# q and k of eight heads in one DRAM tensor, and three V tiles moved between the scores

## The chip, the cores and the metric

The kernel runs on one core of one Trainium2 chip. The metric is the device time of one execution in microseconds (us), the median of several runs. Engines: TensorE (PE for products, PEld for its weight loads), VectorE (DVE), ScalarE (ACT), GpSimd (POOL), and SyncE (SP), which here only issues DMA transfers. SBUF is the memory on the chip with 128 partitions, PSUM the memory that TensorE writes, in banks of 128 x 512 float32; DRAM is the memory off the chip.

## The reference

The inputs are x (1 x 2048 x 512, float32), and weights for attention (wqkv, wo), for a gated MLP (w1, w3, w2; F = 1792) and for a gate (gate_w):

```
q, k, v = split(x @ wqkv)              # 32 heads of 16
p = softmax(q @ k.T * 16 ** -0.5)      # per head, 2048 x 2048
a = merge(p @ v) @ wo
b = (silu(x @ w1) * (x @ w3)) @ w2
g = sigmoid((x * gate_w).sum(-1))
out = g * a + (1 - g) * b
```

## The kernel before

All products run in a float32 mode with each operand split in a high and a low half, hi and lo, and three products in place of one (hi·hi, hi·lo, lo·hi). Only p·V uses plain float32.

The work has three parts.

**The head.** x is loaded and transposed. `project_qk` computes q and k of the first 128 columns, which are 8 heads of 16 (column group c = 0), in four blocks of 512 rows of x (b = 0 to 3). ScalarE writes hi, VectorE lo, and `store_qk` stores them in DRAM. `project_v` computes a tile of V, 128 rows, with 12 full products. The 16 tiles of V fill the time of TensorE while the last block of q and k goes to DRAM and comes back. `bound` and `guard_rows` work out a bound on the scores, and two more rows for q (m_d) that keep the exponent safe. Then a flag is read by all engines, and a branch (`row_maxima`, line 293) is passed whose body runs only for large scores. The last three tiles of V (13 to 15) are computed ahead of the branch and copied behind it (line 415).

**The loop.** The order of all that TensorE does is written out by hand as a string: Q is a score (for two heads at once, 128 keys x 512 queries each), F a slot of other work, P two blocks of p·V. One period holds 8 scores. `one` has 21 slots F, `two` has 15; LONG and SHORT say how often each is used. There are 32 steps of 32 scores (16 pairs of heads, two halves of the queries). `load_step` fetches q, k and the guard rows of the next step when a step is 6 scores old. Each head's operand has 50 rows: three times 16 for the hi and lo combinations (q: hi, lo, hi; k: hi, hi, lo) and two guard rows. So a step took 3 + 3 fetches for each of two heads, and 2 for the guard rows: 14.

In a slot F, `feed` gives one half product (64 of 128 rows of weights) to each of two lanes, which are the halves of TensorE's array. A block of other work takes 12 or so slots in one lane, then as many in the other, and writes one of three PSUM banks. `blocks` lists the blocks in order: q and k of the column groups 1 to 3 (24 blocks, handled by `qk_done`), the MLP's first layer, its second (`h_product`), and the product with wo for the first half of the rows. When a block is done, `qk_done` copies its bank to a buffer `gs` (VectorE, line 443), and POOL makes hi in `sg` and lo in `gs` (lines 444 and 445); then SP stores both. `gs` and `sg` have two buffers each. `pick` gives a bank to a new block when the block three before it was done at least REST = 7 clock steps ago.

SP issues all DMA transfers in the order of the program. Each uses one of eight semaphores in turn, and waits for the one that used it before.

**The tail.** After the last p·V, what is left of the product with wo is done for the tiles 8 to 15; `mix` (VectorE) or `scaled` (ScalarE and POOL) adds the gated parts, and the rows go out.

Of the kernel before, what the change touches and what calls it, by code (L numbers as in the profile page):

```python
# [17 lines left out]
P = 128  # L18
S = 2048
# [3 lines left out]
DH = 16  # L23
NB = S // 512
# [9 lines left out]
def gated_mix_kernel(ctx: ExitStack, tc: tile.TileContext, x, wqkv, wo, w1, w3, w2, gate_w, out):  # L34
# [27 lines left out]
    qkp = ctx.enter_context(tc.tile_pool(name="qkp", bufs=1))  # L62
    fw = ctx.enter_context(tc.tile_pool(name="fw", bufs=2, side="right"))
# [3 lines left out]
    wvp = ph1.enter_context(tc.tile_pool(name="wvp", bufs=1))  # L67

    QD = [[dram.tile([D, S], F32, name=f"{n}{p}_d") for p in "HL"] for n in "qk"]
# [110 lines left out]
    def x_gate(b):  # L180
        for t in range(4):
            nc.vector.scalar_tensor_tensor(slot("hx", F32), xn[b][:, t, :], 1.0, gw, op0=OP.mult, op1=OP.mult,
                                           accum_out=z[:, 4 * b + t:4 * b + t + 1])

    def store_qk(i, c, b, hi, lo):
        for t, d in zip((hi, lo), QD[i]):
            nc.sync.dma_start(d[P * c:P * c + P, 512 * b:512 * b + 512], t.bitcast(F32) if t.dtype == F32R else t)

    def project_qk(c, b, w, between=None):
        ps = psum2()  # L190
        for i in range(2):
            if i and between:
                between()
            order = [(h, xs, k) for h, xs in ((0, xH), (1, xH), (0, xL)) for k in range(ND)]
            if c == b == i == 0:
                order = [(0, xH, 0), (0, xH, 3), (0, xH, 1), (0, xH, 2), (0, xL, 0), (0, xL, 3),
                         (1, xH, 0), (1, xH, 3), (1, xH, 1), (1, xH, 2), (0, xL, 1), (0, xL, 2)]
            for n, (h, xs, k) in enumerate(order):
                nc.tensor.matmul(ps[:, i, :], w[i][h][:, k, :], xs[b][:, k, :], start=n == 0,  # L199
                                 stop=n == len(order) - 1)  # L200
        hi = p1.tile([P, 2, 512], F32R, name="hi", bufs=2)
        lo = p1.tile([P, 2, 512], F32R, name="lo", bufs=2)
        nc.scalar.activation(hi, ps, AF.Copy)
        nc.vector.tensor_sub(lo, ps, hi)
        for i in range(2):
            store_qk(i, c, b, hi[:, i, :], lo[:, i, :])
# [3 lines left out]
    def load_v():  # L210
        for k in range(ND):
            r = slot(("fh1", "fl1", "fh3", "fl3")[k], F32)
            nc.sync.dma_start(r, wqkv[P * k:P * k + P, 2 * D:3 * D])
            vh, vl = (wvp.tile([P, 512], F32R, name=f"v{n}{k}") for n in "hl")
            nc.gpsimd.tensor_copy(vh, r)
            nc.gpsimd.tensor_sub(vl, r, vh)
            wv.append((vh, vl))
# [46 lines left out]

    def load_k(j, i):
        for h in range(2):
            r = 64 * h
            s = slice(DH * (2 * j + h), DH * (2 * j + h) + DH)
            for o, ks in enumerate((0, 0, 1)):
                nc.sync.dma_start(Kt[i][r + DH * o:r + DH * o + DH, :].bitcast(F32), QD[1][ks][s, :])  # L270

    def load_q(j, half, i):
        for h in range(2):
            r = 64 * h
            s = slice(DH * (2 * j + h), DH * (2 * j + h) + DH)
            for o, qs in enumerate((0, 1, 0)):
                nc.sync.dma_start(Qt[i][r + DH * o:r + DH * o + DH, :].bitcast(F32),
                                  QD[0][qs][s, 1024 * half:1024 * half + 1024])

    def load_guard(j, half, i):  # L280
        for h in range(2):
            nc.sync.dma_start(Qt[i][64 * h + 48:64 * h + 50, :].bitcast(F32),
                              M_d[2 * j + h, :, 1024 * half:1024 * half + 1024])
# [154 lines left out]
    def qk_done(c, i, b):  # L438
        def done(ps):
            nonlocal qk_left  # L440
            lo = slot("gs", F32)
            hi = slot("sg")
            nc.vector.tensor_copy(lo, ps)
            nc.gpsimd.tensor_copy(hi, lo)
            nc.gpsimd.tensor_sub(lo, lo, hi)
            store_qk(i, c, b, hi, lo)
            qk_left -= 1
        return done
# [73 lines left out]
    def load_piece(t, q):  # L522
        if t == 1 and q < 2:
            both = wk.tile([P, 2, 512], F32R, name=f"wo{2 + q}")
            hi, lo = both[:, 0, :], both[:, 1, :]
        else:
            hi, lo = (slot(SETS[t % 2][2 * q + i])[:] for i in range(2))
        tag = "fr" if t == 0 or t == 1 and q < 2 else "sg"
        n = min(4, NF - 4 * q)
        src = h_d[512 * q:512 * q + P * n, P * t:P * t + P].rearrange("(f p) t -> p f t", p=P)  # L530
        halves_of(src, hi[:, 0:P * n], lo[:, 0:P * n], tag)
        hs.setdefault(t, []).append((hi, lo))

    def load_wo(k):
        if k < 2:
            hi, lo = w2H[3][:, 2 + k, :], w2L[3][:, 2 + k, :]
        else:
            both = wk.tile([P, 2, 512], F32R, name=f"wo{k}")
# [66 lines left out]
    def divide(k, half):  # L605

        yield from reciprocals(k, half)
        for b in (2 * half, 2 * half + 1):
            for _ in range(5):
                yield  # L610
            if half == 0:
                o, r = slot("hx", F32), slot("gw", F32)
            else:
                both = wk.tile([P, 2, 512], F32, name="od")
# [12 lines left out]
    def load_bt(t):  # L627
        bt[t] = wk.tile([P, 512], F32, name=f"bt{t % 3}")
# [62 lines left out]
    def six_heads():  # L691
# [9 lines left out]
        both = wk.tile([P, 2, 512], F32, name="od")  # L701
# [13 lines left out]

    def blocks():
# [21 lines left out]
    NBLOCK = 8 * len(chunks) + 3 * NT + NT // 2 + NT // 2  # L738
# [4 lines left out]
    halves = [None, None]  # L743
# [7 lines left out]
    def pick(lane, rest, gap):  # L751
# [3 lines left out]
        if used < 0 or over[used] is not None and over[used] + rest <= clock:  # L755
            block, halves[lane] = halves[lane] or next(source, None), None
            if block:
                if type(block[1]) is tuple:
                    product, done, length = block
                    block, halves[1 - lane] = (product, done[0], length), (product, done[1], length)  # L760
                over.append(None)
                return dict(block=block, ps=bank(), id=len(over) - 1, n=0, turn=None, alone=halves[1 - lane] is not None or len(over) == NBLOCK)
# [78 lines left out]
    LONG, SHORT = 90, 37  # L841
# [7 lines left out]
    for i, c in enumerate(order):  # L849
        clock += 1 if c != "P" else 4  # L850
        if c == "Q":
# [14 lines left out]
            if small or later and hurry:  # L866
                for _ in range(3 if hurry else 1 + (len(small) > (6 if len(over) < 8 * len(chunks) - 16 else 0))):
                    if small or later and hurry:
                        (small or later).pop(0)()
            if loads and (hurry or issued % 2 or len(over) > 8 * len(chunks) - 12):  # L870
                loads.pop(0)()
# [44 lines left out]
    project(last, 1, (0, 1))  # L916
# [8 lines left out]
    project(last, 1, (2,))  # L925
    project(last, 2)

    def scaled(t):
        y = wk.tile([P, 512], F32, name=f"p{free[t // 2 - 3]}")
        nc.scalar.activation(y, banks[t], AF.Copy, scale=g[:, t:t + 1])  # L930
        nc.gpsimd.tensor_add(bt[t], bt[t], y)

    def store(t):
        nc.sync.dma_start(out[P * t:P * t + P, :], bt[t])

    banks[8], banks[9] = one_[:, 1, :], two_[:, 1, :]
    banks[10], banks[11] = bank(), bank()
    for two in ((8, 9), (10, 11), (12, 13), (14,), (15,)):
        if two[0] == 12:
            banks[12], banks[13], banks[14] = psum2()[:, 0, :], psum2()[:, 0, :], acc  # L940
        for terms in ((0, 1), (2,)):
            for t in two:
                project(t, k, terms)
        for t in two:
            if t in (8, 10):
                scaled(t)
            elif t < last:
                mix(t, banks[t], nc.scalar if t % 2 == 0 else nc.sync)
                if t in (9, 11):
                    store(t - 1)  # L950
            else:
                mix(t, banks[t], nc.scalar, slice(0, D // 2))
                mix(t, banks[t], nc.sync, slice(D // 2, D))
# [27 lines left out]
```

## Time and profile before

| | |
|---|---|
| median of 3 runs | 1403.08 us (1402.96 to 1403.56) |
| the profiled execution | 1403.71 us, span of its instructions 1401.9 us |
| TensorE busy | 1393.8 us (99%) |
| ScalarE busy | 1034.3 us (74%) |
| VectorE, POOL busy | 486.9 us (35%), 329.3 us (23%) |
| DMA | 112479 packets, 141.03 MB, 101 GB/s on average |
| granted clock of TensorE | 0.999 |

The profile's page gives the busy time of each engine, then the chain of work that ended last: followed back from the last instruction, at each step to what released it. The chain in order of time lists the same pieces with start and length. A timeline lists instructions with start, length, engine, line, what they write and read, and in brackets the idle time before them with what ended it. A view by line lists its instructions with their shortest, median and longest time in ns, and whom they waited for. A window gives the busy time of each engine between two times, then TensorE's clock, the mean busy share of the 16 DMA engines and what they moved. Queues that issue are written SPq, DVEq and so on.

### The profile page before, as it was taken

The numbers are of one execution on the slowest core, as the hardware profiler recorded it, in microseconds if no ns is written. First come the engines' busy times: TensorE is split into PE (matmuls) and PEld (weight loads), VectorE is DVE, ScalarE is ACT, GpSimd is POOL, SyncE is SP. The second block draws the span as 40 slices with busy tenths as digits, with TensorE's granted clock in tenths as the row PEclk, the third lists the DMA queues.
The fourth block names the chain that finished last, engine by engine and source line by source line (L and its number), as shares of the span: only waits on it lengthen the run. The fifth ranks groups of instructions, "written<-read, shape, count | busy, mean of one in ns | idle before, by whom it ended". The sixth has DMA issues, their size and how long they took to land.

```text
span 1401.9 us, 29019 instructions
## 1 busy us (share of the span) xinstructions
PE 1393.8 (99%) x11497; PEld 826.4 (59%) x11497; DVE 486.9 (35%) x1083; ACT 1034.3 (74%) x1155; POOL 329.3 (23%) x366
## 2 busy tenths in 40 slices
PE   9999999999999999999999999999999999999998
PEld 8866566566566566566566566566555555555554
DVE  5511111564555546555454554511111101111113
ACT  4457677777777777777777777777677887888784
POOL 6123433011011101110110116432344322212312
PEclk9999999999999999999999999999999999999999
DMA  7653554343223423223333236444354453444632
GB/s 209 166 124 94 133 139 113 73 113 77 46 56 85 114 54 76 69 66 93 74 77 74 66 86 165 118 95 91 87 123 105 105 110 77 111 93 110 157 120 78
DMA packets 112479, 141.03 MB, mean 101 GB/s; under 512 B 16276, under 2 KB 70804, under 8 KB 109264
## 3 DMA queue, kind: packets, MB, share of 16 engines
q1 hardware_dynamic: 111616, 137.92, 41.4%
q8 instruction: 93, 1.52, 0.5%
q10 hardware_dynamic: 720, 1.18, 0.2%
q14 instruction: 50, 0.41, 0.1%
HBM read 90.43 MB, written 48.61 MB: 99 GB/s over the span
## 4 chain that ended last, share of the span: by engine, by line
PE 99%; DVE 0%; issue 0%; DVEq 0%
PE acc L817 33%; PE f L432 27%; PE S L829 19%; PE f L550 11%; PE f L634 2%; PE S L199 2%; PE f L641 1%; PE f L96 1%; PE f L98 1%; PE f L97 1%; PE f L165 0%; PE acc L353 0%; PE f L897 0%; PE S L165 0%; PE S L897 0%; DVE xL L646 0%
## 5 line engine op out<-in xcount | busy, mean ns | idle before, releaser
L833 ACT ACTIVATE p<-S 128x1024 f32<-128x1024 f32 x1024 | 967.9, 1026 | 314.1 <-PE S L829 305.0
L817 PE MATMUL acc<-p,V 128*17 128x512 f32 x4096 | 471.5, 594 | 0.0
L829 PE MATMUL S<-Qt,Kt 50*128 50x512 f32 x2048 | 403.7, 407 | 0.8 <-DVE V L415 0.8
L829 PEld LDWEIGHTS S<-Qt,Kt 50*128 50x128 f32 x2048 | 184.0, 184 | 173.5 <-issue 77.7
L817 PEld LDWEIGHTS acc<-p,V 128*17 128x17 f32 x4096 | 103.4, 97 | 275.2 <-issue 275.2
L463 DVE RECIPROCAL sg<-sg 128x64 f32<-128x64 f32 x448 | 209.2, 517 | 52.7 <-issue 49.1
L432 PE MATMUL f<-xH,fl 64*128 64x512 f32 x1088 | 220.6, 395 | 0.0
L432 PE MATMUL f<-xL,fh 64*128 64x512 f32 x1088 | 219.6, 393 | 0.0
L432 PE MATMUL f<-xH,fh 64*128 64x512 f32 x1088 | 218.0, 389 | 0.0
L328 POOL CAST fh<-fr 128x512 fp32r<-128x512 f32 x34 | 22.4, 658 | 428.0 <-DMA fr<-in_B_w_dram 279.6
L432 PEld LDWEIGHTS f<-xH,fh 64*128 64x128 f32 x1088 | 105.6, 184 | 25.0 <-issue 0.4
L432 PEld LDWEIGHTS f<-xL,fh 64*128 64x128 f32 x1088 | 106.4, 186 | 22.5
L432 PEld LDWEIGHTS f<-xH,fl 64*128 64x128 f32 x1088 | 106.1, 186 | 22.7
L789 DVE MEMSET tick<- 1x1 f32 x198 | 11.7, 59 | 281.2 <-PE f L550 143.0
L455 DVE COPY gs<-f 128x512 f32<-128x512 f32 x56 | 38.5, 688 | 65.5 <-PE f L432 59.3
L461 DVE TENSOR_SCALAR sg<-sg 128x512 f32<-128x512 f32 x56 | 27.3, 488 | 88.0 <-ACT sg L460 84.3
L550 PE MATMUL f<-xH,fh 64*128 64x512 f32 x208 | 57.5, 392 | 0.0
L550 PE MATMUL f<-xH,raw 64*128 64x512 f32 x192 | 57.0, 392 | 0.0
L550 PE MATMUL f<-xL,fh 64*128 64x512 f32 x208 | 56.2, 392 | 0.0
L550 PE MATMUL f<-xH,fl 64*128 64x512 f32 x208 | 55.4, 392 | 0.0
L513 POOL CAST fh<-sg 128x512 fp32r<-128x512 f32 (+1 forms) x32 | 18.0, 563 | 147.3 <-DMA sg<-h_d 91.0
L799 DVE COPY u<-acc 128x512 f32<-128x512 f32 x31 | 21.4, 692 | 86.1 <-PE acc L817 86.1
(202 smaller groups left out, 1324.6 us busy)
## 6 DMA issues: line engine op xcount, KB each, us to landing
Kt<-kH_d SPq DMA_DIRECT2D x128, 128.0 KB
h_d<-sg SPq DMA_DIRECT2D x56, 256.0 KB
sg<-h_d SPq DMA_DIRECT2D x43, 256.0 KB
fr<-in_B_w_dram SPq DMA_DIRECT2D x42, 256.0 KB
Qt<-qH_d SPq DMA_DIRECT2D x128, 64.0 KB
Kt<-kL_d SPq DMA_DIRECT2D x64, 128.0 KB
Qt<-qL_d SPq DMA_DIRECT2D x64, 64.0 KB
b_d<-y SPq DMA_DIRECT2D x16, 256.0 KB
```

The lines of the kernel that those rows point to most:

```text
L199: nc.tensor.matmul(ps[:, i, :], w[i][h][:, k, :], xs[b][:, k, :], start=n == 0, stop=n == len(order) - 1)
L328: nc.gpsimd.tensor_copy(hi, src)
L432: return nc.tensor.matmul(ps, w[i == 1][r, k, :], (xL if i == 2 else xH)[b][r, k, :], start=n == 0 and not second, stop=n == 3 * ND - 1 an ...
L455: nc.vector.tensor_copy(gs, ps)
L461: small.append(lambda: nc.vector.tensor_scalar(sg, sg, 1.0, None, op0=OP.add))
L463: small.append(lambda q=q: nc.vector.reciprocal(sg[:, q:q + 64], sg[:, q:q + 64]))
L550: ins = nc.tensor.matmul(ps, hs[t][q][i == 1][r, P * o:P * o + P], (w2L if i == 2 else w2H)[q][r, o, :], start=n == 0 and not second, stop ...
L634: return nc.tensor.matmul(ps, ot[t][i == 1][r, P * k:P * k + P], wo_[k][i == 2][r, :], start=n == 0 and not second, stop=n == 3 * ND - 1 a ...
L799: nc.vector.tensor_copy(u, acc)
L817: nc.tensor.matmul(acc[r:r + DH + 1, :], V[:, k, 2 * j + h, :], p[:, h, :], start=k == 0, stop=k == NT - 1)
L829: nc.tensor.matmul(ps[:, h, :], Kt[i][r:r + 50, P * k:P * k + P], Qt[i][r:r + 50, t:t + 512], start=True, stop=True)
L833: nc.scalar.activation(p, ps, AF.Exp, scale=SCALE)
```

## The change

q and k of 8 heads go to one DRAM tensor for each column group, `QK[i][c]`, ordered by o (0 to 2, the copy), then d (the row in a head, 16), then head (8), then 2048 positions. Copy o holds hi or lo as the operand of the score wants it, so hi is stored twice: three stores of 128 x 512 in place of two. A fetch of a head's 48 rows is then one transfer; a step has 2 for q, 2 for k, and 2 for the guard rows.

The tiles 13 to 15 of V leave the head (EARLY = 13) and become the first blocks of the loop's other work. LONG goes from 90 to 96 and SHORT from 37 to 31. `bound` comes ahead of tile 9, and the fetches of the first step come directly one after another behind the guard rows.

The tiles of wv stay in SBUF and lend their place later (`v0` to `v3`) to tiles that had names of their own (wo2, wo3, od, bt). At the end of the loop, tile 13's part is split in the two lanes as tile 14's was, the last three blocks may take a bank after 3 steps instead of 7, and the tail's tiles 8 to 15 are computed and mixed one by one, all on VectorE.

```diff
-    QD = [[dram.tile([D, S], F32, name=f"{n}{p}_d") for p in "HL"] for n in "qk"]
+    QK = [[dram.tile([3, DH, 8, S], F32, name=f"{n}{c}_d") for c in range(ND)] for n in "qk"]
...
-    def store_qk(i, c, b, hi, lo):
-        for t, d in zip((hi, lo), QD[i]):
-            nc.sync.dma_start(d[P * c:P * c + P, 512 * b:512 * b + 512], t.bitcast(F32) if t.dtype == F32R else t)
+    def store_qk(i, c, b, half, t):
+        for o, low in enumerate(((0, 1, 0), (0, 0, 1))[i]):
+            if low == half:
+                nc.sync.dma_start(QK[i][c][o, :, :, 512 * b:512 * b + 512].rearrange("d h t -> h d t"),
+                                  t.bitcast(F32) if t.dtype == F32R else t)
...
+    def rows_of(i, hh):
+        return QK[i][hh // 8].rearrange("o d h t -> (o d) h t")[:, hh % 8, :]
+
     def load_k(j, i):
         for h in range(2):
-            r = 64 * h
-            s = slice(DH * (2 * j + h), DH * (2 * j + h) + DH)
-            for o, ks in enumerate((0, 0, 1)):
-                nc.sync.dma_start(Kt[i][r + DH * o:r + DH * o + DH, :].bitcast(F32), QD[1][ks][s, :])
+            nc.sync.dma_start(Kt[i][64 * h:64 * h + 3 * DH, :].bitcast(F32), rows_of(1, 2 * j + h))
...
     project_qk(0, 3, wq)
+    bound()
+    project_v(9)
+    guard_rows()
     load_q(0, 0, 0)
-    project_v(9)
-    bound()
+    load_k(0, 0)
+    load_guard(0, 0, 0)
+    x_gate(3)
     project_v(10)
-    guard_rows()
-    load_k(0, 0)
-    project_v(11)
-    x_gate(3)
...
-    load_guard(0, 0, 0)
-    project_v(12)
     small = nc.values_load(flag, min_val=0, max_val=1)
-    last_v = [sums_v(t) for t in range(NT - 3, NT)]
+    last_v = [sums_v(t) for t in range(11, EARLY)]
...
+    def v_product(t):
+        b, o = divmod(P * t, 512)
+        def product(ps, r, n, second):
+            k, i = divmod(n, 3)
+            return nc.tensor.matmul(ps, (xL if i == 1 else xH)[b][r, k, o:o + P], wv[k][i == 2][r, :],
+                                    start=n == 0 and not second, stop=n == 3 * ND - 1 and second)
+        return product
...
+        for t in range(EARLY, NT):
+            yield v_product(t), v_done(t), 3 * ND
...
-        for t in range(NT // 2, NT - 2):
+        for t in range(NT // 2, NT - 3):
             yield part_product(t, True), part_done(t), LATE
-        yield part_product(NT - 2, False), (part_done(NT - 2), part_done(NT - 2)), LATE
+        for t in (NT - 3, NT - 2):
+            yield part_product(t, False), (part_done(t), part_done(t)), LATE
...
-    LONG, SHORT = 90, 37
+    LONG, SHORT = 96, 31
...
-    for two in ((8, 9), (10, 11), (12, 13), (14,), (15,)):
-        if two[0] == 12:
+    project(8, k, (0, 1))
+    project(last, 2, (2,))
+    project(8, k, (2,))
+    mix(8, banks[8])
+    for t in range(9, NT):
+        if t == 12:
             banks[12], banks[13], banks[14] = psum2()[:, 0, :], psum2()[:, 0, :], acc
...
```

More of the change, by code (lines that the diff above doesn't have):

```diff
@@ L23 @@
 DH = 16
+EARLY = 13
 NB = S // 512
@@ L204, in project_qk @@
         nc.vector.tensor_sub(lo, ps, hi)
-        for i in range(2):
-            store_qk(i, c, b, hi[:, i, :], lo[:, i, :])
+        for half, t in ((0, hi), (1, lo)):
+            for i in range(2):
+                store_qk(i, c, b, half, t[:, i, :])
     wv = []
@@ L213, in load_v @@
             nc.sync.dma_start(r, wqkv[P * k:P * k + P, 2 * D:3 * D])
-            vh, vl = (wvp.tile([P, 512], F32R, name=f"v{n}{k}") for n in "hl")
+            both = wvp.tile([P, 2, 512], F32R, name=f"v{k}")
+            vh, vl = both[:, 0, :], both[:, 1, :]
             nc.gpsimd.tensor_copy(vh, r)
@@ L445, in done @@
             nc.gpsimd.tensor_sub(lo, lo, hi)
-            store_qk(i, c, b, hi, lo)
+            for half, t in ((0, hi), (1, lo)):
+                store_qk(i, c, b, half, t)
             qk_left -= 1
@@ L627, in load_bt @@
     def load_bt(t):
-        bt[t] = wk.tile([P, 512], F32, name=f"bt{t % 3}")
+        if t == 0:
+            both = wvp.tile([P, 2, 512], F32, name="v3")
+            bt[-3], bt[-2] = both[:, 0, :], both[:, 1, :]
+            bt[-1] = wk.tile([P, 512], F32, name="bt")[:]
+        bt[t] = bt[t - 3]
         nc.sync.dma_start(bt[t], B_d[P * t:P * t + P, :])
@@ L754, in pick @@
         used = len(over) - 3
-        if used < 0 or over[used] is not None and over[used] + rest <= clock:
-            block, halves[lane] = halves[lane] or next(source, None), None
+        if used < 0 or over[used] is not None and over[used] + (rest if len(over) < NBLOCK - 3 else 3) <= clock:
+            alone = bool(halves[lane])
+            block = halves[lane].pop(0) if alone else next(source, None)
             if block:
@@ L759, in pick @@
                     product, done, length = block
-                    block, halves[1 - lane] = (product, done[0], length), (product, done[1], length)
+                    block, alone = (product, done[0], length), True
+                    halves[1 - lane].append((product, done[1], length))
                 over.append(None)
-                return dict(block=block, ps=bank(), id=len(over) - 1, n=0, turn=None, alone=halves[1 - lane] is not None or len(over) == NBLOCK)
+                return dict(block=block, ps=bank(), id=len(over) - 1, n=0, turn=None, alone=alone)
         return None
@@ L866, in gated_mix_kernel @@
             if small or later and hurry:
-                for _ in range(3 if hurry else 1 + (len(small) > (6 if len(over) < 8 * len(chunks) - 16 else 0))):
+                for _ in range(3 if hurry else 1 + (len(small) > (6 if len(over) < FIRST - 16 else 0))):
                     if small or later and hurry:
                         (small or later).pop(0)()
-            if loads and (hurry or issued % 2 or len(over) > 8 * len(chunks) - 12):
+            if loads and (hurry or issued % 2 or len(over) > FIRST - 12):
                 loads.pop(0)()
@@ L915, in gated_mix_kernel @@
     project(last, 0, (1, 2))
-    project(last, 1, (0, 1))
+    project(last, 1)
     rr = slice(PAD, P)
@@ L924, in gated_mix_kernel @@
         nc.vector.tensor_sub(Ol[k][rr, a, :], back[a][rr, :], Oh[k][rr, a, :])
[L925 to L934, printed above, removed]
+    project(last, 2, (0, 1))
     banks[8], banks[9] = one_[:, 1, :], two_[:, 1, :]
     banks[10], banks[11] = bank(), bank()
-    for two in ((8, 9), (10, 11), (12, 13), (14,), (15,)):
-        if two[0] == 12:
-            banks[12], banks[13], banks[14] = psum2()[:, 0, :], psum2()[:, 0, :], acc
[L941 to L953, printed above, removed]
+    project(8, k, (0, 1))
[4 more added lines that the diff above has]
+        if t == 12:
+            banks[12], banks[13], banks[14] = psum2()[:, 0, :], psum2()[:, 0, :], acc
+        project(t, k)
+        if t < last:
+            mix(t, banks[t], nc.scalar if t % 2 else nc.sync)
+        else:
+            mix(t, banks[t], nc.scalar, slice(0, D // 2))
+            mix(t, banks[t], nc.sync, slice(D // 2, D))
 _INS = ['A_x', 'A_wqkv', 'A_wo', 'B_w1', 'B_w3', 'B_w2', 'gate_w']
```

32 lines of the change are left out of this document (16 added, 16 removed).

## The prediction

> **What bounds the kernel now.** I read the page first (shares, chain), then the chain in order of time, then the timeline of the last 20 us before the loop, then windows of DMA load.
>
> ```profile
> span 1401.9 us, 29019 instructions
> PE 1393.8 (99%) x11497; PEld 826.4 (59%) x11497; DVE 486.9 (35%) x1083; ACT 1034.3 (74%) x1155; POOL 329.3 (23%) x366
> PE 99%; DVE 0%; issue 0%; DVEq 0%
> L829 PE MATMUL S<-Qt,Kt 50*128 50x512 f32 x2048 | 403.7, 407 | 0.8 <-DVE V L415 0.8
> Kt<-kH_d SPq DMA_DIRECT2D x128, 128.0 KB
> Qt<-qH_d SPq DMA_DIRECT2D x128, 64.0 KB
> ```
>
> The chain is TensorE almost alone, and in the whole run the scores waited 0.8 us, once. No fetch of q or k is ever late, so eight fetches fewer a step shorten nothing by themselves: the fetches lie beside TensorE's work. Time comes only from TensorE's work moving, or from a new wait.
>
> ```profile
> 88.08 3.56 PE acc L817 x32
> 98.57 3.56 PE acc L817 x32
> ...
> 1023.33 3.56 PE acc L817 x32
> ...
> 1034.07 1.84 PE acc L817 x16
> 1043.50 1.84 PE acc L817 x16
> ...
> 1373.14 1.84 PE acc L817 x16
> ```
>
> These are pieces of the chain, the p·V products once a period. From 88.08 to 1023.33 lie 89 periods of the string `one`: 10.508 us each. From 1034.07 to 1373.14 lie 36 of `two`: 9.419 us each. The pace holds to a few hundredths: the loop has no stalls to win back.
>
> **Step 1: the V tiles leave the head.** Now the last 20 us before the loop.
>
> ```profile
> 61.36 0.34 SPq L187 DMA_DIRECT2D qH_d<-hi  x1
> 61.37 1.23 DVE L204 TENSOR_TENSOR lo<-S,hi 128x1024 fp32r<-128x1024 f32 x1 [1.75 <-ACT hi L203]
> 63.49 0.45 SPq L187 DMA_DIRECT2D kL_d<-lo  x1
> 66.09 0.27 PE L255 MATMUL f<-top,V 1*32 1x1 f32 x2
> ...
> 71.43 0.17 DVE L408 TENSOR_SCALAR omg<-g 128x16 f32<-128x16 f32 x1
> 73.37 0.55 SPq L282 DMA_DIRECT2D Qt<-m_d  x2
> 76.72 1.49 DVE L415 COPY V<-f 128x512 f32<-128x512 f32 x2 [5.12 <-DVEq L293]
> 77.09 0.39 PE L98 MATMUL f<-vh,xL 128*128 128x512 f32 x1
> 79.81 0.39 PE L98 MATMUL f<-vh,xL 128*128 128x512 f32 x1
> 80.97 0.93 PE L829 MATMUL S<-Qt,Kt 50*128 50x512 f32 x4 [0.78 <-DVE V L415]
> ```
> ```profile
> L293 SPq EVENT_SEMAPHORE  x8: 17/17/17, 78.5 to 79.1; - x8
> L293 SPq COMPARE_BRANCH  x1: 50/50/50, 75.2 to 75.2; - x1
> ```
>
> One V tile is 12 products: 77.09 to 79.81, 2.72 us. Three leave: 8.2 us. If nothing else were late, the first score would start at 80.97 - 8.2 = 72.8. Three things must now be ready that much earlier:
>
> DVE. From the small product of line 255 to line 408 it takes 5.5 us (66.09 to 71.60), and the branch of line 293 holds it 5.1 us more. In the new order `bound` comes ahead of tile 9 and that product at about 63.3 (after lo, 62.60, and DVE's short maxima): the two V copies end at about 75.5. They hold the bank of the second lane of work, so 75 is near the earliest start of the loop.
>
> SP. Its last fetch is issued by 73.92, its semaphores behind the branch come at 78.5 to 79.1: 5.2 us. Now it issues 14 DMAs ahead of the branch (6 stores, 2 for m_d, 6 fetches) where it issued 20, but each of the last waits for room behind the stores; I keep 5.2 us, so this ends no later than the data below.
>
> The transfers themselves:
>
> ```profile
> 62.20:66.20 4.00, 4.00 (x21) 2.71 (x19) 1.09 (x5) 0.60 (x2) 0.71 (x1) 1.00 0.93 259
> 66.20:70.70 4.50, 4.50 (x21) 3.74 (x22) 4.00 (x11) 1.22 (x3) 0.00 (x0) 1.00 0.99 204
> 70.70:75.80 5.10, 5.10 (x24) 4.20 (x24) 0.60 (x3) 0.80 (x2) 0.00 (x0) 1.00 0.99 164
> 117.35:118.15 0.80, 0.80 (x10) 0.67 (x8) 0.00 (x0) 0.80 (x2) 0.80 (x1) 1.00 0.99 364
> 615.00:616.20 1.20, 1.20 (x16) 0.27 (x12) 0.00 (x0) 0.00 (x0) 0.00 (x0) 1.00 0.52 191
> 84.00:230.00 146.00, 146.00 (x1250) 88.16 (x1249) 20.04 (x51) 104.58 (x112) 56.43 (x60) 1.00 0.53 129
> ```
>
> Windows; the last two columns are the busy share of the 16 DMA engines and GB/s. From 62.2 to 75.8 the DMA engines are full (0.93 to 0.99): four stores in 4.0 us, then 9.6 us for guard rows, q and k. That was covered by TensorE until 80.2; with three tiles fewer it is not.
>
> **Step 2: how wide a store is.** The new store writes DRAM as `h d t`, outermost 8 heads, then 16, where the old one wrote 128 rows. One transfer of the kernel already has this shape: line 603 fetches R_d as 8 x 16 x 512.
>
> ```profile
> L603 SPq DMA_DIRECT2D gw<-r_d x8: 595/602/617, 278.2 to 812.8; - x8
> L601 SPq DMA_DIRECT2D hx<-o_d x8: 343/415/459, 277.7 to 811.8; - x8
> L187 SPq DMA_DIRECT2D qH_d<-sg x12: 319/344/1225, 95.2 to 224.0; - x12
> ```
>
> It costs SP 602 ns where its neighbour of 128 rows and the same size costs 415. While it runs alone (615.00 to 616.20) the engines are busy 0.52 and move 191 GB/s; while a store of 128 rows runs alone (117.35) they are busy 0.99 and move 364. I read this as eight of the sixteen engines. A store of 256 KB then takes 262144 / 191 GB/s = 1.37 us of those eight instead of 0.72 of all; where four stood in a row the rate was 259, half of it 130: 2.0 us. Bounds 1.37 and 2.0 each; I take 1.6.
>
> [...]
>
> Head: six stores now, 8.2 to 12 us, then the rest: at most the 9.6 us of before, at least, with the other eight engines done early, half of its 1.7 MB at 191 GB/s, 4.5 us. So the data is there between 74.9 and 83.8. I take 78.5, in the middle, as the stores run one behind another. First score 2.5 us earlier (range 6 earlier to 3 later).
>
> **Step 3: 36 slots more in the loop.** LONG goes up by 6 and SHORT down by 6: 6 x (10.508 - 9.419) = 6.5 us. They hold the 36 slots (12 for each tile, two half products a slot) at less than 36 times a full product, since `two` has a second change between p·V and scores. Other strings between q and k work move by 36 slots, nothing else.
>
> **Step 4: 72 narrow stores in the first 146 us of the loop.** The loop writes 24 blocks of q and k. Before, two stores each, 48 x 0.72 = 35 us of all engines. Now hi goes twice, three stores: 72 x 1.37 = 99 to 72 x 2.0 = 144 us of eight engines. The stage (84 to 230) had share 0.53, 77 us; without its stores 43 us. Together 142 to 187 us in 146: these eight engines are full or over-full. What waits for them:
>
> ```profile
> L443 DVE COPY gs<-f x24: 691/692/694, 93.8 to 226.4; 128x512 f32<-128x512 f32 x24
> ...
>   DMA kL_d<-gs: 11.0, 3
> ...
> L445 POOL TENSOR_TENSOR gs<-gs,sg x24: 1266/1291/1302, 95.3 to 227.9; 128x512 f32<-128x512 f32 x24
> ```
>
> `gs` and `sg` have two buffers each. The copy of line 443 that empties a PSUM bank must wait until the store of two blocks ago has landed; it did so already (11.0 us in 3 waits, while TensorE did not stall). Behind the copy on DVE stand the small memsets that let the other lane start, and in the queue of SP everything that comes later; TensorE, in order, stops at the next product into that bank, scores included. The order reuses a bank from 7 clock steps after its block, about 1.6 us at the 0.23 of a product (2.72 / 12), and the copy takes 0.7, so a copy may be under 1 us late. Below: at 1.37 us a store, and fetches no slower than now, the engines just keep up: 0. Above: 187 - 146 = 41 us. At 1.6: 115 + 43 - 146 = 12 us. I take 12.
>
> [...]
>
> **Step 5: the rest.** The three V copies (0.69 us) and the moved `x_gate`, `bound`, guard rows lie on DVE beside TensorE; DVE is busy 35%. Tiles that change their place in SBUF (wo, od, bt) are filled hundreds of us after their predecessors are done: nothing; without that cover, one landing of 2 to 3 us.
>
> The tail:
> ```profile
> L646 DVE SCALAR_TENSOR_TENSOR xH<-S,g,xH x1: 751/751/751, 1392.1 to 1392.1; 128x512 f32<-128x512 f32 x1
> L930 ACT ACTIVATE p<-S,g x1: 687/687/687, 1391.9 to 1391.9; 128x512 f32<-128x512 f32 x1
> 1386.14 0.66 PE f L641 x2
> ```
> Splitting tile 13 too leaves one more slot after the strings (0.23). Tiles 8 and 10 go from ACT and POOL to DVE: eight mixes in a row at 0.75 against three products at 0.70, so DVE becomes the last engine; against that mixing starts some 0.4 earlier. Together +0.5 (0 to +1).
>
> **Sum:** -2.5 + 6.5 + 12 + 0.5 = +16.5 on the span of 1401.9 (its run took 1403.71 against the median of 1403.08): 1419 on the median.
>
> **Rivals.**
> (a) The buffers absorb the stores (1.37 us each, quicker fetches): -3.5 + 6.5 + 1 + 0.5 = +4.5, 1407.5. For it: the lower bound fills the engines to 142 of 146. Against: fetches come in bursts of 5 us (70.70 to 75.80), against less than 1 us of slack.
> (b) Saturation at 2.0 us: 0 + 6.5 + 35 + 0.5, 1445. For it: the rate with four stores in a row. Against: half as many engines may meet less contention.
> (c) Not slower: stores keep all engines. The stage then has 72 x 0.72 + 43 = 95 of 146 us and no stall. In the head six stores at the pace of now end at 68.2 and the rest at 77.8, or at 75 if k comes twice as fast; TensorE, free from 72.8, waits 2 to 5 us: -8.2 + 2 to 5 + 6.5 + 0.5 = +0.8 to +3.8, 1404 to 1407. For it: SBUF's side of the store still has 128 rows. Against: line 603's has too. It decides when a new store costs no more than 1 us and the first score starts before 77.
>
> **How the numbers follow.** The forecast of step 4 (stall of 3 to 28 us) 0.54; (a) 0.18; (b) 0.11; (c) 0.14; faster by something unseen 0.03. A measurement tells about 0.2%, 2.8 us, from no change. Of (c) 0.11 lies within it, the rest and the other cases are slower: faster 0.03, same 0.11, slower 0.86. The range from 1404 to 1440 leaves out most of (b) and the lower edge of (c).
>
> **What would show it.** First score near 78.5, with TensorE idle some 5 us before it; stores of q and k at 0.6 us issue, DMA share near 0.5 while only they run; between 80 and 270 us TensorE waits for line 443's copy, and that for landings of the `gs` stores, largest behind a step's fetches; periods of 10.5 and 9.4 us elsewhere; eight mixes in a row on DVE at the end. I am wrong if a store of the new shape keeps a share near 0.99, or if TensorE has no waits in that stage.

## The result and the profile after

The median is 1449.4 us after (1445.9 to 1452.7) and 1403.6 before: a ratio of 1.0328, with a 95% interval of 1.0311 to 1.0345. The change makes the kernel 46 us slower; the forecast was 1419. The profiled execution after took 1448.34 us with a span of 1446.3. Its page, span and busy times, the chain by engine, and the fetches:

```profile
span 1446.3 us, 28807 instructions
PE 1407.9 (97%) x11533; PEld 834.7 (58%) x11533; DVE 488.3 (34%) x1090; ACT 1032.7 (71%) x1151; POOL 325.8 (23%) x364
PE 85%; DMA 4%; issue 2%; POOL 2%; SPq 1%; DVE 0%; POOLq 0%; DVEq 0%
Kt<-k_d SPq DMA_DIRECT2D x64, 384.0 KB
Qt<-q_d SPq DMA_DIRECT2D x64, 192.0 KB
```

The chain was 99% TensorE and is 85% now; DMAs and POOL have come into it. TensorE's busy time grew too, by 14 us (1393.8 to 1407.9), and its mean granted clock fell from 0.999 to 0.987. The four largest waits of TensorE, with the total in us, the number of waits and the longest:

```profile
PE f L432 <- DVE tick L811: 12.5, 4, 4.7
PE S L851 <- SPq L295: 7.6, 1, 7.6
PE f L250 <- DVE rs L244: 6.5, 1, 6.5
PE f L551 <- POOL fr L514: 3.5, 1, 3.5
```

Before, the list had 0.8 us of a score; a wait of 1.6 us near the start (1.5 after) is in both. Each row is a place: the products of q and k in the loop (line 432), the first score (line 851), the norms of the weights in the head (line 250), and the products with h near 970 us (line 551). The chain in order of time:

```profile
91.15 1.42 PE S L851 x4
...
1125.68 3.56 PE acc L839 x32
...
1428.37 3.56 PE acc L839 x32
```

The first score starts at 91.15 (80.97 before). The first product with V is at 99.96 (88.02 before; 100.03 in the chain), the 96th at 1125.68, the last at 1428.37, the end 17.9 behind it. With 95 periods of 10.508 between first and 96th, 27.4 us are left over: stalls. Added up against before: first score +10.2; from there to the first product with V +1.8 (8.8 instead of 7.0); stalls +27.4; six periods of `one` for six of `two` +6.5; the tail -1.4. That is 44.4, the difference of the spans. The same numbers for the kernels below, from the trace of one execution each (stalls are what periods take beyond 10.508, those of the q and k stage up to 270 us, those of the h products from 920 on; the medians are of all executions, among them one of 1967 us in e11; the traced execution of e12 is its fastest, 1404.7 us):

| kernel | first score | to first V product | stalls, q/k stage | stalls, h | span | median |
|---|---|---|---|---|---|---|
| before | 80.97 | 7.04 | 0 | 0 | 1401.9 | 1403.6 |
| after | 91.15 | 8.81 | 20.2 | 6.4 | 1446.3 | 1449.4 |
| e1 V part alone | 80.36 | 9.47 | 0 | 10.3 | 1423.1 | 1423.2 |
| e2 q/k part alone | 93.69 | 9.58 | 11.3 | 0 | 1428.7 | 1431.3 |
| e3 wide stores | 79.24 | 8.95 | 0 | 8.8 | 1416.3 | 1418.0 |
| e4 narrow, rows 8 KB apart | 92.87 | 9.29 | 24.5 | 10.0 | 1457.1 | 1458.8 |
| e5 wide, step 21 later | 77.73 | 9.50 | 0 | 0.5 | 1409.2 | 1410.9 |
| e6 e5, TensorE kept busy | 83.12 | 8.55 | 0 | 0.6 | 1413.4 | 1415.7 |
| e7 wide in the head | 78.63 | 8.57 | 18.1 | 7.7 | 1433.2 | 1437.2 |
| e8 more buffers | 91.11 | 9.59 | 0 | 6.6 | 1428.1 | 1430.3 |
| e9 wide, no V part | 86.24 | 9.16 | 0 | 0 | 1409.6 | 1411.4 |
| e10 e9 and new tail | 85.11 | 8.49 | 0 | 0 | 1406.5 | 1407.8 |
| e11 e9, step 1 later | 83.11 | 8.50 | 0 | 0 | 1405.9 | 1407.2 |
| e12 e10, step 1 later | 82.50 | 7.05 | 0 | 0 | 1402.5 | 1406.4 |
| e13 e11, code moved | 80.65 | 7.64 | 0 | 0 | 1402.5 | 1404.6 |
| e14 tail alone | 81.22 | 7.09 | 0 | 0 | 1403.5 | 1405.1 |

### The profile page after: what moved, and what is told of

It reads as the page before. It is cut to its first block, busy times and chain, and to the rows that moved or that the text cites. A ratio compares the mean times of both kernels' runs of the same rounds, so it can differ in the third digit from the quotient of the medians.

```text
span 1446.3 us, 28807 instructions
## 1 busy us (share of the span) xinstructions
PE 1407.9 (97%) x11533; PEld 834.7 (58%) x11533; DVE 488.3 (34%) x1090; ACT 1032.7 (71%) x1151; POOL 325.8 (23%) x364
## 4 chain that ended last, share of the span: by engine, by line
PE 85%; DMA 4%; issue 2%; POOL 2%; SPq 1%; DVE 0%; POOLq 0%; DVEq 0%
PE acc L839 30%; PE f L432 24%; PE S L851 17%; PE f L551 10%; PE f L639 2%; DMA q_d<-sg 1%; PE f L646 1%; DMA k_d<-gs 1%; PE f L725 1%; POOL gs L445 1%; DMA sg<-h_d 0%; DMA q_d<-gs 0%; POOL sg L444 0%; DMA k_d<-sg 0%; PE f L919 0%
## 5 line engine op out<-in xcount | busy, mean ns | idle before, releaser
L432 PE MATMUL f<-xH,fl 64*128 64x512 f32 x1088 | 221.0, 399 | 12.5 <-DVE tick L811 12.5
L551 PE MATMUL f<-xH,fr 64*128 64x512 f32 x160 | 51.7, 395 | 4.4 <-POOL fr L514 3.5
```

The lines of the kernel that those rows point to most:

```text
L432: return nc.tensor.matmul(ps, w[i == 1][r, k, :], (xL if i == 2 else xH)[b][r, k, :], start=n == 0 and not second, stop=n == 3 * ND - 1 an ...
L551: ins = nc.tensor.matmul(ps, hs[t][q][i == 1][r, P * o:P * o + P], (w2L if i == 2 else w2H)[q][r, o, :], start=n == 0 and not second, stop ...
```

## Experiments

Theory 1: the narrow stores cost the time, in the head and in the loop. Rivals: the new order and the V tiles (2), the bytes of the third store (3), rows 64 KB apart (4). The first four runs part the change and vary one thing of a store.

**e1, the V part alone.** Tensors, two stores and 14 fetches as before:

```diff
-    QK = [[dram.tile([3, DH, 8, S], F32, ...) for c in range(ND)] for n in "qk"]
+    QD = [[dram.tile([D, S], F32, ...) for p in "HL"] for n in "qk"]
```

> The kernel after with the DRAM tensors, stores (two of 128 rows a block and operand) and 14 fetches a step of before: the V tiles, the head's order, the strings and the tail alone. Theory 1 (the narrow stores cost the time: eight engines each, in the head and in the loop): only the strings' +6.5, the tail's -1.4 and a head that ends 0 to 6 us earlier are left: 1402 to 1409, no period of the loop longer than 10.6 us. Rival 2 (the new order of the head stalls TensorE by itself: bound ahead of tile 9, three tiles less to hide q and k): first score near 91 as after, 1413 to 1420. Rival 3 (the third store's bytes): as theory 1.

1423.2 us, ratio 1.0138 (1.0121 to 1.0155). None of the three fits: the head is as short as theory 1 has it, but a stall of 10.3 us stands where nobody had put one, in the h products. TensorE's two largest waits of this run:

```profile
PE S L851 <- SPq L295: 7.5, 1, 7.5
PE f L551 <- POOL fr L514: 6.2, 1, 6.2
```

SP's queue and POOL around it (start, duration, what):

```profile
924.05 1.12 SPq L827 DMA_DIRECT2D d_d<-u  x4
925.21 1.69 SPq L833 DMA_DIRECT2D o_d<-u  x4
...
928.41 0.45 SPq L483 DMA_DIRECT2D h_d<-sg  x1
932.51 0.37 SPq L513 DMA_DIRECT2D sg<-h_d  x1
932.98 0.45 SPq L279 DMA_DIRECT2D Qt<-qH_d  x1
...
939.36 8.86 SPq L513 DMA_DIRECT2D sg<-h_d  x3
```
```profile
945.87 0.61 POOL L514 CAST fr<-sg 128x512 fp32r<-128x512 f32 x1 [8.27 <-DMA sg<-h_d]
```

The pieces of h that the first two tiles of products need go out behind the copies of a step's end and the 14 fetches of the next step; POOL gets the data at 945.87, TensorE wanted it at 940. In before the same pieces stood ahead of them:

```profile
906.73 0.33 SPq L482 DMA_DIRECT2D h_d<-sg  x1
909.04 5.12 SPq L512 DMA_DIRECT2D sg<-h_d  x3
922.64 1.12 SPq L805 DMA_DIRECT2D d_d<-u  x4
```

Putting 36 slots of V ahead of all other work moved that work by 1.7 periods of 21 slots against the steps, which are tied to the scores.

**e2, the q and k part alone.** Before, with the new tensors, stores and fetches:

```diff
-            store_qk(i, c, b, hi, lo)
+            for half, t in ((0, hi), (1, lo)):
+                store_qk(i, c, b, half, t)
```

> The kernel before with the new tensors, three narrow stores and 6 fetches a step, and nothing of the V part. Theory 1: the loop's stall of 20 to 30 us is there, the head is covered in part by the three V tiles (0 to +8), no +6.5: 1424 to 1440. Rival 2 (order of the head and V part): 1404 to 1412. Rival 3 (the third store's bytes, at any width): as theory 1.

1431.3 us, ratio 1.0202 (1.0185 to 1.0219), as theory 1 said; its head is later than said (+12.7 with three tiles of V to cover it), its stalls fewer (11.3).

**e3, wide stores.** The columns of the weights are put in the order (row, head) when they are split:

```diff
-        nc.gpsimd.tensor_copy(wh, w)
+        nc.gpsimd.tensor_copy(as_row(wh), by_row(w))
...
-    nc.sync.dma_start(QK[i][c][o, :, :, 512 * b:512 * b + 512].rearrange("d h t -> h d t"), ...)
+    nc.sync.dma_start(QK[i][c][o].rearrange("d h t -> (d h) t")[:, 512 * b:512 * b + 512], ...)
```

> The kernel after, with the columns of the q and k weights put in the order (row, head) when they are split, so that a block of 128 partitions is stored as 128 consecutive rows; still three stores a block, 57 MB written, and the same 6 fetches of 48 rows. Theory 1: the stores go by all sixteen engines, no stall in the loop, first score 74 to 82: 1400 to 1408. Rival 3 (the third store's bytes and its hold on gs and sg): 24 stores more at about 0.72 us and a stage that waits for them: 1425 or more. Rival 4 (the fetches from rows 64 KB apart are what is slow): 1430 or more, as the fetches stay.

1418.0 us, ratio 1.0099 (1.0082 to 1.0116): 31 us less than after by nothing but the width. The head and the q and k stage are as theory 1 said, with as many bytes and the same fetches: rivals 3 and 4 fall. The 10 us above its range are the h stall of e1 and the slow clock behind the first score (0.50 between 78 and 82; 8.95 us to the first product with V instead of 7.04). What a store does to the DMA engines, in windows that hold little else (the last two columns are their busy share and GB/s; a packet counts whole where it starts, so a share can pass 1), narrow in after, then wide:

```profile
171.50:175.50 4.00, 4.00 (x37) 1.96 (x30) 0.00 (x0) 1.32 (x2) 0.26 (x1) 1.00 0.52 180
```
```profile
118.50:121.00 2.50, 2.50 (x28) 1.08 (x28) 0.69 (x2) 2.38 (x3) 0.12 (x1) 1.00 1.04 379
```

**e4, narrow with rows 8 KB apart.** One row of padding a head, 14 fetches:

```diff
-    QK = [[dram.tile([3, DH, 8, S], F32, ...) ...
+    QK = [[dram.tile([3, 8, DH + 1, S], F32, ...) ...
...
+                nc.sync.dma_start(QK[i][c][o, :, 0:DH, 512 * b:512 * b + 512], ...)
```

> The kernel after with tensors ordered by head, then row, with one row of padding for each head, so that the rows of a head lie 8 KB apart: three stores a block of 8 x 16 rows (eight engines each), 14 fetches a step of 16 rows as before. Theory 1: as after, 1435 to 1455. Rival 4 (rows 64 KB apart, in stores or fetches, are what is slow): 1400 to 1412. Rival 3: as theory 1.

1458.8 us, ratio 1.0398 (1.0381 to 1.0415): as slow as after and 9 us more, so the distance of the rows is not it. The 9 us lie in all pieces of the table; whether they come from 14 fetches behind narrow stores or from the padding stays open.

The next four take the pieces apart.

**e5, the fetch of step 21 later** (on e3):

```diff
-            if issued % 32 == 6 and step < 2 * NPAIR:
+            if issued % 32 == (16 if step == 21 else 6) and step < 2 * NPAIR:
```

> The kernel with wide stores (the columns of the weights reordered), in which the fetch of step 21 alone is issued 10 scores later, after the pieces of h for the first two tiles of the h products. Theory 2 (moving 36 slots into the loop put the last products of the gate stage behind the end of step 20, so that the first pieces of h queue behind that step's copies and the fetch of step 21): the wait of 4.7 us for fr near 940 and the slow clock after it shrink, 2 to 9 us less than the kernel with wide stores: 1409 to 1416. Rival (POOL's order, w2 ahead of the pieces, or the eight copies to D_d and O_d are it, not the fetch): unchanged, 1417 to 1419.

1410.9 us, ratio 1.0045 (1.0028 to 1.0062); the h stall goes from 8.8 to 0.5. It was the place in SP's queue.

**e6, TensorE kept busy ahead of the loop** (on e5):

```diff
     last_v = [sums_v(t) for t in range(11, EARLY)]
+    idle(36)
```

> As the kernel before this one, and 36 transposes of 0.11 us more on TensorE behind the last V tile, where it stands idle from 73.0 to 79.2 while SP and DVE come out of the branch. Theory 3 (an idle TensorE of some 4 us loses half of its granted clock for the next 5 us): the granted clock stays at 1.00 up to the loop, first score 79 to 80, first product with V 7.0 to 7.3 us behind it rather than 8.95: 1 to 2 us less in all. Rival (TensorE's branch comes 3.9 us later and holds the first score, or the clock falls whatever TensorE does): first score at 81 or later, or 8.9 us as now; 0 to 3 us more.

1415.7 us, ratio 1.0086 (1.0070 to 1.0103): 4.8 us more than e5, beyond the rival's 0 to 3. TensorE's branch came behind the transposes, as the rival has it, at 75.2 instead of 67.9, and the first score at 83.1. The clock still fell, about 2.5 us into an idle time of 5.8 us (to 0.50 between 80 and 82). Whether a TensorE that never idles keeps its clock was not tested by it; e11 and e12 below bear on that.

**e7, wide in the head only.** The order of columns is changed for c = 0 alone:

```diff
+                d = QK[i][c][o, :, :, 512 * b:512 * b + 512]
+                nc.sync.dma_start(d.rearrange("d h t -> (d h) t" if c == 0 else "d h t -> h d t"), ...)
```

> The kernel after, with the columns of the first 128 columns of the q and k weights alone reordered: the head's four blocks are stored 128 rows wide, the loop's 24 blocks narrow as in after. Theory 1: the head ends as with wide stores, first score 79 to 80 instead of 91.1; the stalls of the loop between 130 and 270 us stay at about 20 us, and the wait in the h stage: 1435 to 1440. Rival (the late head is caused by the order of the head, and wide stores help only in the loop): first score at 88 or later, 1446 or more. Rival (a loop that starts early finds the stores of the loop no longer in its way): below 1428.

1437.2 us, ratio 1.0244 (1.0227 to 1.0261): first score 78.6, stalls of the loop as in after. The 24 stores of the head alone cost 12.5 us there. SP's queue in after:

```profile
32.52 7.43 SPq L126 DMA_DIRECT2D fr<-in_A_wqkv_dram  x3
...
55.41 4.06 SPq L126 DMA_DIRECT2D fr<-in_A_wqkv_dram  x3
```

and in before:

```profile
27.50 6.96 SPq L125 DMA_DIRECT2D fr<-in_A_wqkv_dram  x3
...
48.89 1.65 SPq L125 DMA_DIRECT2D fr<-in_A_wqkv_dram  x3
```

The weights of q and k are fetched behind the stores of the first three blocks, and their fetches are issued 5.0 and 6.5 us later. The last step of their norms starts at 66.8 instead of 57.2 (57.9 in e7). In ScalarE's part of the program the squares of these weights, then of four tiles of x, stand ahead of hi of the last block. After, and then before:

```profile
64.45 0.63 ACT L243 ACTIVATE raw<-fr 128x512 f32<-128x512 f32 x1 [8.17 <-DMA fr<-in_A_wqkv_dram]
...
69.11 1.00 ACT L206 ACTIVATE hi<-S 128x1024 fp32r<-128x1024 f32 x1
```
```profile
60.31 1.03 ACT L203 ACTIVATE hi<-S 128x1024 fp32r<-128x1024 f32 x1 [0.89 <-PE S L199]
```

TensorE had its products for that block by 61.1, but hi came 8.8 us later than before (in e7 it comes at 61.1), and the last block's stores go out from 70.1 instead of 61.4. `bound` waits for the norms too, ahead of the V tiles, and so does TensorE (6.5 us on line 250).

**e8, more buffers in the loop.** Stores and fetches as in after:

```diff
-            lo = slot("gs", F32)
-            hi = slot("sg")
+            lo = slot(("gs", "raw", "gs", "raw", "raw")[qk_left % 5], F32)
+            hi = slot(("sg", "hx", "sg", "gw")[qk_left % 4])
```

> The kernel after, in which the loop's q and k blocks take turns over five buffers for lo and four for hi instead of two and two; stores and fetches as in after. Theory 1 in the form predicted (the copy out of PSUM waits for the landing of the store two blocks ago): most of the 20 us of stalls between 130 and 270 us go, the head and the h stage stay: 1428 to 1436. Rival (the eight engines or SP's queue are full for so long that buffers only put it off; or SP, in order, is what waits): 1444 to 1450.

1430.3 us, ratio 1.0189 (1.0172 to 1.0206): the stalls of the q and k stage are gone, all 20.2 us. What DVE's copy of line 443 waited for, after and then e8:

```profile
  DMA q_d<-gs: 28.5, 4
  PE f L432: 18.8, 8
  DMA k_d<-gs: 15.3, 3
```
```profile
  PE f L432: 37.8, 18
  issue: 12.1, 5
  DMA o_d<-u: 0.9, 1
```

A piece of after's chain shows how long one such landing takes:

```profile
146.77 7.47 DMA k_d<-gs
```

Six stores of a pair of blocks land some 1.4 us one behind the other (172.4, 174.0, 175.6, 176.9, 178.3, 179.6), the first 4.0 us behind its issue and the others 5.0 to 6.5 (issued from 168.35 to 173.35); the landings in the chain of this stage come 5.0 to 7.5 us behind their issues, and the copy two blocks on wants its buffer sooner. Most of the loss in after lies in three periods, near 142, 202 and 249 us, which are 6.4, 4.2 and 7.8 us longer; the other pairs cost under 1 us. The transfers as such fit into the stage: with five and four buffers nothing waits.

The last six look for a version worth keeping, and for what still stood ahead of the loop.

**e9, wide stores and 6 fetches, no V part** (before with e3's layout). 

> The kernel before with the new tensors, wide stores (columns of the weights reordered), three stores a block and 6 fetches a step, and nothing of the V part. Theory (in the kernel before, no fetch of q or k is late, so eight fetches fewer a step and the third store, both beside TensorE, change nothing): first score 80 to 81.5, no stalls in the loop: 1402.5 to 1405. Rival (the third store of each block fills gs and sg longer and stalls the loop): 1407 or more. Rival (the fetches were worth something): below 1401.5.

1411.4 us, ratio 1.0049 (1.0035 to 1.0063): slower, against the theory. There is no stall in the loop; the first score comes at 86.2, after an idle time that the profile puts down to a small fetch; the one that lands then is the next step's, which these scores don't use:

```profile
PE S L837 <- DMA Qt<-m_d: 6.0, 1, 6.0
```

**e10, e3 without V tiles in the loop, with the new tail:** `EARLY = 16`, `LONG, SHORT = 90, 37`, the head's order as before. 

> The kernel after with wide stores, with all V tiles and the order of the head as before (no V tile in the loop, LONG 90) and the new tail alone. Theory: what is left of the change is the tail's -1.4 and the layout at nothing: 1401 to 1403, the one version that is not slower than before. Rival (the tail's gain came from the V part, as its slots end elsewhere): 1403.5 to 1405.

1407.8 us, ratio 1.0030 (1.0018 to 1.0041): the same wait, 4.2 us.

DMA queues in a window, with packets, MB and share: e9 between 80 and 82, e9 between 83 and 85, and before between 80 and 82. `q8` is of kind "instruction", 16 KB a packet; that it brings TensorE's code is an assumption here, which e13 bears out.

```profile
q1 hardware_dynamic: 87, 0.48, 117.2%
```
```profile
q8 instruction: 1, 0.02, 4.8%
```
```profile
q1 hardware_dynamic: 88, 0.20, 37.9%
q8 instruction: 1, 0.02, 3.5%
```

In before the packet starts at 80.4, as TensorE comes out of the branch. There SP spreads the fetch of step 1 over 14 DMAs from 79.2 to 86.2. In e9 it has put out the same fetch by 80.3, 1168 KB in six DMAs (768 of them k; the text of e11 below counts k alone); the packet starts at 83.5, ends at 85.0, and the first score follows at 86.2. Theory 4: TensorE waits for its code.

**e11, on e9, and e12, on e10, the fetch of step 1 later:**

```diff
-            if issued % 32 == 6 and step < 2 * NPAIR:
+            if issued % 32 == (18 if step == 1 else 6) and step < 2 * NPAIR:
```

> The kernel with the new tensors, wide stores and 6 fetches a step but without the V part, in which the fetch of step 1 alone is issued after 18 scores instead of 6. There TensorE stood idle 6.0 us ahead of the first score though q, k and the last V tile were there. Theory 4 (TensorE waits for 16 KB of its own instructions, whose packet queues behind the 768 KB of the fetch of step 1, issued in 2.6 us right behind the branch): the packet starts within 0.5 us of 80.2 as in the kernel before, first score 80.9 to 82, 1403 to 1405. Rival (a wait on a semaphore or the code itself holds it, whatever the engines do): first score 85 or later, 1409 to 1412.

> The kernel with wide stores, all V tiles ahead of the loop and the new tail, with the fetch of step 1 issued after 18 scores as well. Theory 4 and the tail's -1.4: first score 81.5 to 82.5 (its V tiles end 0.7 us later than before), 1402.3 to 1404. Rival: first score 85 as without the later fetch, 1406.5 to 1408.5.

1407.2 us (1.0022, 1.0013 to 1.0031) and 1406.4 us (1.0019, 1.0011 to 1.0028). e11 is between its two forecasts; e12's median is at the rival's lower end, while its traced execution, the fastest, has the first score that theory 4 gave. The packets start at 80.8 and 80.3, the first scores at 83.1 and 82.5: 2.9 and 2.2 us of wait are left, which end 1.3 to 1.4 us behind the packet's end.

**e13, the place of the code** (on e11): the line `idle(10)` is left out, ten transposes into a scratch bank. 

> The kernel without the V part, wide stores, 6 fetches, fetch of step 1 after 18 scores, in which the ten transposes that TensorE does into a scratch bank while it waits for x (1.0 us near 7.6) are left out: some 20 of its instructions fewer ahead of the branch, so that all its later code lies 20 instructions earlier in the packets of 16 KB. Theory 4 (TensorE ran out of code four instructions behind the branch, and the packet asked for at 80.2 came at 81.7): TensorE runs on for some 20 instructions, about 2 us, and the wait of 2.9 us ahead of the first score shrinks to under 1 us, there or behind the first scores: 1403.5 to 1405. Rival (the wait is the branch's own and goes with the number of fetches and semaphores, wherever the code lies): 2 to 3 us of wait as before, 1406.5 to 1408.

1404.6 us, ratio 1.0007 (0.9998 to 1.0017), as theory 4 said. The code ahead of the branch is some 20 instructions shorter, and the wait is gone; TensorE's waits of e11 and then of e13 at the first score:

```profile
PE S L837 <- issue: 2.9, 1, 2.9
```
```profile
PE S L836 <- PEq L299: 0.5, 1, 0.5
```

**e14, the tail alone** (before's tensors, V tiles and head, after's tail). 

> The kernel before with the tail of after alone: tensors, stores, 14 fetches, V tiles and order of the head as before. Theory: the tail's -1.4 stands by itself, first score 80.5 to 81.5, 1401.5 to 1402.5, the one part of the change that is worth keeping. Rival (the tail's gain is offset by the slot and the half that it puts into the loop, or its tiles' places in SBUF): 1403 to 1404.5.

1405.1 us, ratio 1.0010 (1.0001 to 1.0019): above both forecasts. Behind the last product with V come 19.8 us here, not 18.0 as in after, e10 and e12. Up to the end of the last mix the tails of e12 and e14 are alike (14.7 us); then SP waits longer for the last store to land. SP's waits from 1396 us on, e14 and then e12, and the code queue in e14 between 1394 and 1397:

```profile
SPq L987 <- DMA out_dram<-xL: 3.4, 2, 3.1
```
```profile
SPq L994 <- DMA out_dram<-xL: 1.7, 2, 1.4
```
```profile
q8 instruction: 1, 0.02, 3.4%
```

One 16 KB packet of code came among the output's stores and took 1.6 us (3.4% of 16 engines in 3 us); in e12 none comes there, and SP's waits are 1.7 us shorter. e6 is the only other kernel with the new tail and a packet at that place, and its tail takes 19.6. So the 1.7 us go with the place of the code; no run moves the packet alone. In e10 and e12 the tail's 1.4 us stand without the V part, against e10's rival. No version beat the kernel before.

The granted clock (the column ahead of the DMA share) behind an idle time ahead of the first score, e11 (2.9 us) and then e12 (2.2 us):

```profile
82.00:84.00 2.00, 0.89 (x5) 0.82 (x7) 0.00 (x0) 0.00 (x0) 0.00 (x0) 0.90 0.00 0
84.00:86.00 2.00, 2.00 (x12) 1.79 (x12) 0.00 (x0) 1.94 (x2) 0.00 (x0) 0.50 0.04 8
```
```profile
84.00:86.00 2.00, 2.00 (x20) 1.93 (x18) 0.00 (x0) 2.00 (x3) 0.00 (x0) 1.00 0.04 8
```

## Why the prediction was wrong

- **The sign and the mechanism of step 4 were right:** stores of the new shape keep the engines half busy and move half as much (0.52 and 180 GB/s against 1.04 and 379; that this is eight of the sixteen engines is read from the share alone), and DVE's copy waits for the landing of the store two blocks ago. Rival (c) is out.
- **The stall's size failed: 12 forecast, 20.2 measured.** The price of a store (1.6) was near the 1.4 between landings. The sum "115 + 43 - 146" was the wrong one: it asks whether the engines keep up over the stage, and by e8 they do. The loss is a landing 5.0 to 7.5 us behind its issue when stores go out in groups of six or three, against two buffers, and after each longer wait a few us at a lower clock (0.50 between 156 and 160 and between 260 and 264, 0.95 on average between 140 and 260), for which the forecast had no term.
- **"Head: six stores now" failed: -2.5 forecast, +10.2 measured,** +12 with the slow clock. Its sum starts at 62.2, with the last block's stores going out as before; they went out from 70.1. From there to the first score it took 21.0 us (19.6 before), so 8.8 of the 10.2 us are the late start. The forecast priced the last block's stores and left out the 18 of the three blocks ahead of it, which are as narrow and stand ahead of the weights' fetches in SP's queue, and with these fetches ScalarE came late to the last block. Moving `bound` ahead of tile 9 is not the cause: in e2, where it keeps its place, hi of the last block comes at 68.0 and the first score at 93.7. e7 gives the price of the head's 24 narrow stores: 12.5 us. Even with wide stores the first score comes at 77.7 to 79.2, 1.7 to 3.2 us sooner, not the 8.2 that TensorE saves: the profile puts its wait down to SP at the branch's line in e3 and e7 (6.1 and 5.8 us), and in e5 to DVE's copy of V behind the branch (5.6).
- **"Other strings between q and k work move by 36 slots, nothing else" failed:** 6.4 us in after, 10.3 in e1. This was an edit costed at nothing without its cover named; the cover was the order of SP's queue near a step's end.
- **The strings' +6.5 held** (10.508 and 9.419 again).
- **The tail came out at -1.4 instead of +0.5** in after, and again in e10 and e12; in e6 and e14, with a packet of code among the last stores, the gain is gone. The forecast had only the mixes in its sum. These end 0.3 us sooner behind the last product with V (14.7 instead of 14.9); the rest lies behind them, where the last store lands.
- **The fetches were worth nothing,** as said. Rival (a) counts on quicker fetches and (c) on k coming twice as fast; no run shows that factor, and little of a gain: between 68.2 and 77.0 e9 moved 166 GB/s and before 155 (DMA shares 0.73 and 0.87).
- **Rival (b) named nearly the time after, 1445,** but by other terms: it had no loss in the head, 35 us of full engines, and no h stall.

In short, of the 44.4 us of span: narrow stores in the head 12.5 (e7), in the loop 20.2 (e8), the place of the h pieces 6.4 (e5 takes nearly all of its like away), the strings 6.5, the tail -1.4. The rest nearly cancels: a head that without its narrow stores ends 2.3 sooner, 1.8 of slow clock behind the first score (0.50 between 90 and 94), 0.7 of smaller stalls.

## What to carry to other kernels

When a store's shape changes, price every store of that shape in the program, and first those that stand ahead of something's fetch in the same queue; follow that fetch to the engine that needs it, and ask what this engine has to do next. Then compare one burst's last landing with the number of buffers, not the mean rate with the stage. Work that is put in front of an order shifts everything behind it against whatever is tied to another count (here the steps, tied to scores): look at each place where the two meet. And look at what is issued in one go right behind a branch: in e9 it was 1168 KB, and the packet read here as TensorE's code started at 83.5 instead of 80.4.

## What the runs showed of the hardware that was not expected

- Packets of 16 KB come on a queue of kind "instruction" of their own (`q8`, 93 packets and 1.52 MB in before). That they bring TensorE's code is the reading of theory 4, which e13 bears out. Behind 1168 KB of data issued in 2.8 us a packet started 3 us later than in before (83.5 instead of 80.4), in a wait of 6.0 us ahead of the first score (e9). With no other packet between 80 and 82, 2.9 us of wait were left (e11), and with some 20 instructions fewer ahead of the branch 0.5 (e13): 2.6 us between the medians of these two. A packet among the last stores went with 1.7 us more at the end (e14, and 1.6 in e6).
- An idle time of 2.9 us ahead of the loop was followed by a granted clock of 0.50 between 84 and 86 (e11), one of 2.2 us was not (1.00 in e12); in e6 the clock fell about 2.5 us into the idle time (0.95 between 78 and 80, 0.50 from 80 to 82, idle from 77.3). After the longer waits, from the first score to the first product with V it took 8.5 to 9.6 us instead of 7.0.
- A late landing can be named by the profile as the cause of a wait that it has nothing to do with (the 6.0 us of e9): its fetch was the next step's.
